# Attention and a two-layer network on one core: nine chunks of 512 tokens in place of 36 of 128, longer load rows, and a hand-set order

## The chip, the cores and the metric

One core of one Trainium2 chip. The metric is the device time of one execution in microseconds (us), lower is better. Every kernel below ran several times, on the same chip and in the same session as the kernel before it. The sessions were on different chips, and the kernel before took 407.98 to 409.81 us in them, so a difference of 1 or 2 us between medians of two sessions says nothing; there the ratios are to be compared.

Names in the profiles: PE is TensorE, which multiplies matrices, PEld its weight loads; DVE is the vector engine, ACT the scalar engine, POOL GpSimd, and SP the sync engine, which here only issues loads and stores. A "y copy" is DVE's copy of a finished y out of the buffer that TensorE writes to.

## The reference, cut to what matters

```python
batch, n_heads, seq, head_dim = 8, 8, 576, 64
n_tokens, d_model, d_ff = 4608, 512, 2048
q_s = np.exp(q - np.max(q, axis=-1, keepdims=True)); q_s = q_s / (np.sum(q_s, axis=-1, keepdims=True) + 1e-09)
k_s = np.exp(k - np.max(k, axis=2, keepdims=True));  k_s = k_s / (np.sum(k_s, axis=2, keepdims=True) + 1e-09)
kv = np.einsum('bhsd,bhse->bhde', k_s, v)             # one 64x64 matrix per head
attn_out = np.einsum('bhsd,bhde->bhse', q_s, kv)
x = attn_out.transpose(0, 2, 1, 3).reshape(B * S, H * D)
h = x @ w_in
g = 0.5 * h * (1.0 + erf(h * inv_sqrt2))
out = g @ w_out
```

There are some 36.7 MB to read and 9.4 MB to write. Nearly all the arithmetic is in the two products of the network, called h and y below. Attention is the part before them; its "kv step" makes the small matrix of each head.

## The kernel before

The network runs in 36 chunks of 128 tokens. In a chunk, four quarters of h (16 matmuls of 128 columns each) alternate with GELU on the scalar engine and four y matmuls of 512 columns. A scheduler chooses the order of instructions on every engine. All input loads are issued from POOL in rows of 256 bytes (64 floats of one head), and the weights pass through two staging buffers of 512 KB.

```python
def load_weights():
    for i in range(NDM):
        for hlf in range(2):
            wtmp = f32in.tile([128, DF // 2], FP32, tag="wtmp")      # pool with bufs=2
            nc.gpsimd.dma_start(out=wtmp, in_=moe_w_in[...])
            nc.scalar.copy(out=wi_bf[:, i, ...], in_=wtmp)
    # ... w_out the same way, cast by nc.vector
def moe_chunk(tcn):
    cols = slice(tcn * 128, (tcn + 1) * 128)
    for qt in range(NQT):                                  # four quarters
        h_ps = psum_m.tile([128, 4, 128], FP32, tag="h", bufs=2)
        for j in range(4):
            t = qt * 4 + j
            for dm in range(NDM):
                nc.tensor.matmul(h_ps[:, j, :], wi_bf[:, dm, t*128:(t+1)*128], xT[dm][:, cols], ...)
        nc.scalar.activation(out=g[:, qt*4:(qt+1)*4, :], in_=h_ps, func=AF.Gelu)
        for j in range(4):
            nc.tensor.matmul(y_ps, g[:, qt*4+j, :], wo_bf[:, qt*4+j, :], ...)
    nc.vector.tensor_copy(out=y_sb, in_=y_ps)
    nc.sync.dma_start(out=out[cols, :], in_=y_sb)
def load_bhsd(dst, src_b, engine):                         # engine: nc.gpsimd
    for c in range(C):                                     # rows of 64 floats
        engine.dma_start(out=dst[:, c, :, :], in_=src_b[:, s0:s0+128, :].rearrange("h p d -> p h d"))
# ... attn_batch(b): exp, sums, multiply by 1/sum, kv step, transposes, products (cut)
```

The softmax here doesn't subtract the row's maximum and nothing guards it: scores larger than these inputs give would overflow.

## Time and profile before

| | before |
|---|---|
| time, median of 4 runs of the session that compared the two | 407.98 us |
| profiled span | 409.1 us |
| TensorE matmuls | 3488 records, busy 84% of the span |
| first GELU | 50.2 us |
| one undisturbed chunk of 128 tokens | 8.08 us |

The page of the kernel before, its slices: the span is cut into 40 equal parts of 10.2 us, each digit is the busy share of a part in tenths, PEclk the granted TensorE clock in tenths, and GB/s what the DMA engines moved.

```profile
span 409.1 us, 7832 instructions
...
PE   0073378998799999999889899999999999989995
...
PEclk9999998996899999999989999999999999999998
...
GB/s 152 218 149 236 207 246 243 229 237 170 137 239 64 203 232 119 239 110 212 221 117 242 88 44 36 28 26 53 27 27 26 53 27 27 27 26 27 27 34 44
...
PE 46%; ACT 21%; DMA 13%; POOL 11%; DVE 5%; issue 4%; ACTq 0%; POOLq 0%
```

TensorE (PE) does nothing in the first two slices (20 us), has 3 to 7 tenths in the next four, where it works on the attention of the first batch and waits for weights, and is at 0.8 or 0.9 nearly everywhere after that. A digit of 9 doesn't say that the engine is at its best. The last line is the share of each engine in the chain of waits that ended last: ACT has 21% of it, in a kernel whose matmuls should bound it. Where it enters is seen in the timeline of one quarter. Columns: start, duration, engine, line and operation, output and inputs, count; in brackets the idle time of the engine before it and what ended it.

```profile
401.49 0.60 ACT L93 ACTIVATE g<-h_ps 128x512 bf16<-128x512 f32 x1 [1.41 <-PE h_ps L86]
402.14 0.55 PEld L98 LDWEIGHTS <-g 128*128 128x128 bf16 x4 [0.25 <-ACT g L93]
402.15 1.04 PE L98 MATMUL y_ps<-wo_bf,g 128*128 128x512 bf16 x4
402.81 0.48 PEld L86 LDWEIGHTS <-wi_bf 128*128 128x128 bf16 x5
403.02 0.44 PE L86 MATMUL h_ps<-xT,wi_bf 128*128 128x128 bf16 x5
403.50 0.60 ACT L93 ACTIVATE g<-h_ps 128x512 bf16<-128x512 f32 x1 [1.41 <-PE h_ps L86]
404.15 0.55 PEld L98 LDWEIGHTS <-g 128*128 128x128 bf16 x4 [0.86 <-ACT g L93]
```

The five h matmuls at 403.02 are the last of their group of 16; the scheduler had put the other eleven ahead of the y group before. Only after them can GELU start (403.50), and y's weight load (404.15) waits for it to end. This is the end of the kernel, with no h left to do in the meantime, and the wait is 0.86 us. Everywhere else eleven matmuls of the next group fill 11 x 56 ns = 0.62 us of it, and about 0.25 us remain, as at 402.14: in the undisturbed stretch 0.25 to 0.31 us in each quarter of 2.007 us. Its sum is in the list of waits (columns: who waits, for what, total us, times, longest).

```profile
PEld L98 <- ACT g L93: 33.5, 110, 2.5
```

### The profile page before, as it was taken

What the parts mean: (1) busy time and instruction counts of PE and PEld (TensorE: products, weight loads), DVE (VectorE), ACT (ScalarE), POOL (GpSimd) and SP (SyncE); (2) the same over time, 40 slices, a digit from 0 to 9 for tenths busy, and PEclk for the clock granted to TensorE, in tenths of its full rate; (3) what the DMA queues carried; (4) which work ended last, traced back from release to release, by engine and by line L of the source; (5) the groups of instructions that cost most, each with busy time, mean ns of one, the idle gap of its engine ahead of it and who ended that gap; (6) DMA issues with size and microseconds to landing.
All of it is one profiled execution on the core that took longest, in us unless ns stands there. A gap on an engine that the chain in (4) does not pass through costs nothing.

```text
span 409.1 us, 7832 instructions
## 1 busy us (share of the span) xinstructions
PE 341.9 (84%) x3488; PEld 228.1 (56%) x3488; DVE 122.9 (30%) x228; ACT 168.7 (41%) x198; POOL 161.4 (39%) x158
## 2 busy tenths in 40 slices
PE   0073378998799999999889899999999999989995
PEld 0041257565466665666646566666666666656663
DVE  0352034256337173490741830011001000250010
ACT  0523563645475293762845822223332322212221
POOL 9753336993955949759397210000000000000000
PEclk9999998996899999999989999999999999999998
DMA  6947678996592894948949310001000100000001
GB/s 152 218 149 236 207 246 243 229 237 170 137 239 64 203 232 119 239 110 212 221 117 242 88 44 36 28 26 53 27 27 26 53 27 27 27 26 27 27 34 44
DMA packets 17121, 49.79 MB, mean 122 GB/s; under 512 B 2752, under 2 KB 2752, under 8 KB 17088
## 3 DMA queue, kind: packets, MB, share of 16 engines
q0 software_dynamic: 11904, 39.85, 39.8%
q1 hardware_dynamic: 5184, 9.44, 6.3%
q8 instruction: 27, 0.44, 0.5%
q14 instruction: 6, 0.05, 0.0%
HBM read 39.85 MB, written 9.44 MB: 120 GB/s over the span
## 4 chain that ended last, share of the span: by engine, by line
PE 46%; ACT 21%; DMA 13%; POOL 11%; DVE 5%; issue 4%; ACTq 0%; POOLq 0%
PE y_ps L98 29%; ACT g L93 15%; PE h_ps L86 11%; DMA wtmp<-in_moe_w_in_dram 5%; PE kv_ps L155 3%; POOL qf L112 3%; POOL qs L139 3%; DMA wtmp<-in_moe_w_out_dram 3%; DMA qf<-in_q_dram 3%; POOL vf L112 2%; DMA vf<-in_v_dram 2%; POOL kf L112 2%; PE ot L182 1%; DVE qsum L136 1%; ACT L93 1%
## 5 line engine op out<-in xcount | busy, mean ns | idle before, releaser
L86 PEld LDWEIGHTS <-wi_bf 128*128 128x128 bf16 x2304 | 145.9, 101 | 48.8 <-ACT wi_bf L60 12.2
L86 PE MATMUL h_ps<-xT,wi_bf 128*128 128x128 bf16 x2304 | 158.6, 224 | 15.2 <-ACT wi_bf L60 11.1
L98 PE MATMUL y_ps<-wo_bf,g 128*128 128x512 bf16 x576 | 150.2, 388 | 17.7 <-ACT g L93 5.1
L93 ACT ACTIVATE g<-h_ps 128x512 bf16<-128x512 f32 x144 | 84.5, 597 | 186.6 <-PE h_ps L86 186.4
L98 PEld LDWEIGHTS <-g 128*128 128x128 bf16 x576 | 47.3, 99 | 76.8 <-ACT g L93 33.5
L106 DVE COPY y_sb<-y_ps 128x512 f32<-128x512 f32 x36 | 24.9, 691 | 186.5 <-PE y_ps L98 186.5
L139 POOL TENSOR_TENSOR qs<-eq,recq 128x2560 bf16<-128x2560 bf16 x8 | 35.8, 4474 | 45.8 <-DVE recq L137 39.5
L112 POOL DMA_DIRECT2D qf<-in_q_dram x40 | 40.8, 1024 | 0.3 <-issue 0.3
L112 POOL DMA_DIRECT2D kf<-in_k_dram x40 | 36.2, 913 | 0.7 <-issue 0.7
L112 POOL DMA_DIRECT2D vf<-in_v_dram x40 | 35.2, 887 | 1.8 <-PE ot L182 1.0
L167 PE MATMUL tp<-identity,qs 128*128 128x128 bf16 x128 | 14.1, 232 | 22.3 <-POOL qs L139 22.3
L188 DVE CAST xT<-ot 128x288 bf16<-128x288 f32 x64 | 26.3, 452 | 12.5 <-PE ot L182 12.2
L155 PE MATMUL kv_ps<-v_aug,ek 128*64 128x65 bf16 (+1 forms) x320 | 28.6, 211 | 0.1
L136 DVE TENSOR_REDUCE qsum<-eq 128x40 f32<-128x2560 bf16 x8 | 22.4, 2805 | 14.3 <-ACT eq L127 14.3
L155 PEld LDWEIGHTS <-ek 128*64 128x64 bf16 (+1 forms) x320 | 20.7, 114 | 10.5 <-issue 5.1
L182 PE MATMUL ot<-qsT,kvn 64*64 64x288 bf16 x128 | 15.5, 321 | 8.1 <-DVE kvn L162 7.9
L167 PEld LDWEIGHTS <-qs 128*128 128x128 bf16 x128 | 7.8, 101 | 24.6 <-POOL qs L139 22.3
L93 ACT ACT_TABLE_LOAD x15 | 19.2, 1283 | 5.2 <-PE h_ps L86 5.0
L128 ACT ACTIVATE ek<-kf 128x2560 bf16<-128x2560 f32 x8 | 18.7, 2337 | 2.4 <-DMA kf<-in_k_dram 2.4
L132 DVE CAST v_aug<-vf 128x2560 bf16<-128x2560 f32 x8 | 17.0, 2130 | 6.7 <-DMA vf<-in_v_dram 6.7
L127 ACT ACTIVATE eq<-qf 128x2560 bf16<-128x2560 f32 x8 | 18.7, 2337 | 0.1
L127 ACT ACT_TABLE_LOAD x8 | 10.3, 1283 | 18.1 <-DMA qf<-in_q_dram 18.0
(19 smaller groups left out, 83.5 us busy)
## 6 DMA issues: line engine op xcount, KB each, us to landing
qf<-in_q_dram POOLq DMA_DIRECT2D x40, 256.0 KB, 4.9
kf<-in_k_dram POOLq DMA_DIRECT2D x40, 256.0 KB, 6.8
vf<-in_v_dram POOLq DMA_DIRECT2D x40, 256.0 KB, 8.6
out_dram<-y_sb SPq DMA_DIRECT2D x36, 256.0 KB, 2.1
wtmp<-in_moe_w_in_dram POOLq DMA_DIRECT2D x8, 512.0 KB, 4.9
wtmp<-in_moe_w_out_dram POOLq DMA_DIRECT2D x8, 512.0 KB, 4.3
```

Of the source, the lines that this page charges most:

```text
L86: nc.tensor.matmul(h_ps[:, j, :], wi_bf[:, dm, t * 128:(t + 1) * 128], xT[dm][:, cols], start=(dm == 0), stop=(dm == NDM - 1),)
L93: nc.scalar.activation(out=g[:, qt * 4:(qt + 1) * 4, :], in_=h_ps, func=AF.Gelu)
L98: nc.tensor.matmul(y_ps, g[:, t, :], wo_bf[:, t, :], start=(t == 0), stop=(t == NDF - 1),)
L106: nc.vector.tensor_copy(out=y_sb, in_=y_ps)
L112: engine.dma_start(out=dst[:, c, :, :], in_=src_b[:, s0:s0 + 128, :].rearrange("h p d -> p h d"),)
L127: nc.scalar.activation(out=eq, in_=qf, func=AF.Exp)
L136: nc.vector.reduce_sum(out=qsum, in_=eq, axis=mybir.AxisListType.X)
L139: nc.gpsimd.tensor_tensor(out=qs, in0=eq, in1=recq.to_broadcast([128, C, H, D]), op=mybir.AluOpType.mult,)
L155: nc.tensor.matmul(kv_ps[pb:pb + 64, :], lhsT, rhs, start=(c == 0), stop=(c == C - 1),)
L167: nc.tensor.transpose(tp[:, c * 128:(c + 1) * 128], qs_flat[:, c, h0 * D:(h0 + 2) * D], identity,)
L182: nc.tensor.matmul(ot[pb:pb + 64, :], kvn[pb:pb + 64, :], qsT[pb:pb + 64, ssl], start=True, stop=True,)
L188: nc.vector.tensor_copy(out=xT[hp][:, b * S + half * 288: b * S + (half + 1) * 288], in_=ot,)
```

## The change

Its intent: (1) work on 512 tokens at a time, h for all 16 groups first, then y for four times 128 tokens, with three h buffers; (2) let a partition hold four neighbouring tokens, so that a load row is 1 KB (the token order is permuted inside a chunk and undone by the store); the last 64 tokens of each batch become a ninth chunk; (3) issue all loads from SP; weights in 1 MB pieces; (4) the two heads of a pair in one kv matmul; (5) switch the scheduler off and set the order on every engine by hand. Cut to its core:

```diff
+    ctx.enter_context(tc.manual_schedule())
+    src = q[b, :, 0:M, :].rearrange("h (p j) d -> p h (j d)", j=J)         # J = 4, M = 512
+    nc.sync.dma_start(out=qf[:, i*n:(i+1)*n, :], in_=src[:, i*n:(i+1)*n, :])
+    def h_phase(c, ins):
+        for t in range(NDF):
+            ps = psum_h.tile([128, M], FP32, tag="h")                      # bufs=3
+            for dm in range(NDM):
+                nc.tensor.matmul(ps, wi_bf[:, dm, t*128:(t+1)*128], xT[:, dm, :], ...)
+            nc.scalar.activation(out=g[:, t, :], in_=ps, func=AF.Gelu)
+            for f in ins.get(t, []): f()                # work set in after group t
+    def y_phase(c, ins):
+        for j in range(J):
+            for t in range(NDF):
+                nc.tensor.matmul(ps, g[:, t, j*128:(j+1)*128], wo_bf[:, t, :], ...)
+                for f in ins.get((j, t), []): f()
+            nc.vector.tensor_copy(out=y_sb, in_=ps)     # then the store
+    wst = ctx.enter_context(tc.tile_pool(name="wst", bufs=2))              # weight staging, 1 MB
+    h_phase(0, ins_h0)
+    exp_k(1); exp_q(1); table(AF.Gelu)
+    y_phase(0, {
+        (0, 15): [lambda: load_q(2), lambda: load_kv(2)],
+        (1, 15): [lambda: norm_q(1, parts=2, engs=[nc.gpsimd, nc.vector]), lambda: cast_v(1)],
+        (2, 15): [lambda: kv_step(1, 0), lambda: kv_step(1, 1), lambda: tp_step(1, 0), lambda: tp_step(1, 1)],
+        (3, 7): [lambda hp=hp: x_step(1, hp, ...) for hp in range(HP)],
+    })
+    # ... chunk 1 alike; for chunks 2 to 8 the attention of the next chunk is set into h,
+    #     and its sums and v cast into y at (1, 15)
-    # ... moe_chunk, load_bhsd, attn_batch, load_weights as above
```

## The prediction

> **What bounds it now.** TensorE, in three stretches (stretch table and timeline):
> - 0 to 50 us: no bulk matmuls. Exp starts at 10.7 us; weights come as 512 KB loads through two buffers (4.7 us from issue to landing); first GELU at 50.2 us. The first loads run at about 215 GB/s (256-byte rows), the DMA engines 85% busy.
> - 50 to about 200 us: 128-token chunks mixed with attention and waits; POOL (120 input-load issues of 0.9 us, 4.5 us multiplies) and DMA are busy.
> - The pure stretch: a chunk takes 8.08 us (y copies at 332.42 and 340.51). A quarter of it is 2.007 us: 16 h matmuls at 56 ns and 4 y matmuls at 217 ns are 1.77; the rest is y's weight load waiting 0.25 to 0.31 us for GELU. 36 x 8.08 = 291 us.
>
> **After (estimates from these rates).** 1152 matmuls of 512 columns at 217 ns, each with its own weight load as y has today: 250 us. The bubble (0.25 x 144 = 36 us) should vanish: GELU takes 0.60 us, four matmuls 0.87, with three PSUM buffers. Attention: about 3.2 us a batch (20 kv matmuls, 16 transposes, 4 of 512), 23 us beyond the start. The Trainium skill ("TensorE: Matmul & The Clock Gate", Part 1) gives 215.7 and 55.6 ns for warm matmuls of 512 and 128 columns; the trace agrees within 1%. So width alone saves nothing; the bubble and the schedule do.
>
> **Start.** 3.4 MB of q, k, v in 1 KB rows: I estimate 300 GB/s (between today's 215 and up to 340 in the weight stretch), v landed at 13 to 15 us, first weights at 17 to 18, then casts and x evictions: h starts at about 21 us, in place of 50. A cold clock costs 1 to 2 us.
>
> **New waits.** (a) Chunk 0's y: batch 1's loads sit on SP behind weight loads that wait for casts and land near 50 us; exps, sums and the v cast follow (2.3, 2.8, 2.1 us for 2560 columns, times 0.8). TensorE, in order, waits about 9 us at batch 1's kv step. (b) Chunk 1's y: batch 2's exps start only after the last GELU; about 6 us at its kv step. (c) Chunks 2 to 5: the DVE block (sums, v cast) stands ahead of the second y copy, whose buffer the fourth y group needs: 1.8 us each, 7 us. (d) Late w_out in chunk 0: 0 to 2 us.
>
> **Sum.** 21 + 1.5 + 250 + 23 + 9 + 6 + 7 + tail 4 (today 3.9 from the last y matmul to the end) = 321; some waits may be hidden: **318 us**, range **302 to 340** (8 in 10). Faster by over 2%: 0.97; within 2%: 0.02; slower: 0.01. Of the 89 us gained, 29 come from the start, 36 from the bubble, the rest from attention waiting less.
>
> **Right if:** first GELU at 20 to 24 us; h and y matmuls at 217 ns in runs of 64; an undisturbed chunk of 27.8 us plus 3.2 of attention; the waits list shows TensorE waiting for DVE (v cast, y copies) some 20 us in all, mostly before 110 us; about 300 GB/s in the first 14 us.
>
> **Wrong if:** 512-column h matmuls don't hide their weight loads; y waits for its chunk's last GELU (0.7 us x 9); 1 KB loads are slower, or SP issues them slowly; the clock drops in the long waits; or POOL and DVE slow each other (the v cast took 1.50 us alone, 2.13 on average).

## The result, and the profile after

326.56 us median of 4 runs, against 407.98 us. The ratio is 0.7984, 95% interval 0.7951 to 0.8017. Here and below a ratio is the mean time of one kernel's fast runs over that of the kernel before in the same rounds, so it isn't quite the ratio of the medians.

The same lines of the page, after (a slice is now 8.1 us):

```profile
span 324.5 us, 3715 instructions
...
PE   0499774799939999999999998999899999999994
...
PEclk9999969599969999999999999999999999999999
...
GB/s 226 329 282 337 306 287 295 298 129 265 95 32 67 162 280 44 65 200 254 34 67 275 177 34 93 283 143 33 105 123 1 65 67 0 26 73 32 0 67 65
...
PE 63%; DVE 11%; ACT 10%; DMA 10%; issue 3%; SPq 2%; POOL 0%; DVEq 0%; ACTq 0%
```

TensorE begins in the second slice, and ACT's share of the chain has fallen from 21 to 10%. But DVE's share has gone from 5 to 11%, and the granted clock drops to 0.6 and 0.5 of full in the sixth and eighth slice and to 0.6 in the twelfth. After the first slice, the loads run at about 300 GB/s (282 to 337) through the eighth; before, no slice had more than 250. The start is now full of data. The table of stretches shows where: start; h of chunk 0; y of chunk 0; chunk 1; chunk 2; chunk 3. Columns: the stretch, its length, busy time of PE, its weight loads, DVE, ACT and POOL, each with its count of instructions, granted clock, DMA share, GB/s.

```profile
0.00:20.00 20.00, 6.83 (x41) 4.14 (x42) 10.95 (x26) 9.68 (x12) 8.37 (x19) 1.00 0.90 275
20.00:35.20 15.20, 15.10 (x62) 6.54 (x64) 4.90 (x6) 10.24 (x17) 2.98 (x2) 1.00 0.86 307
35.20:68.20 33.00, 21.75 (x104) 11.10 (x104) 13.74 (x24) 8.90 (x10) 5.16 (x4) 0.79 0.99 280
68.20:106.60 38.40, 32.41 (x167) 16.14 (x168) 14.23 (x25) 20.67 (x25) 1.90 (x1) 0.91 0.42 117
106.60:137.80 31.20, 30.68 (x167) 15.04 (x169) 16.63 (x26) 16.55 (x22) 9.42 (x2) 1.00 0.51 143
137.80:169.40 31.60, 30.79 (x167) 15.05 (x169) 12.79 (x23) 16.55 (x22) 4.71 (x1) 1.00 0.51 142
```

A chunk with attention needs, by the rates of the prediction, 27.8 + 3.2 = 31.0 us; chunks 2 and 3 take 31.2 and 31.6. But y of chunk 0 with the attention of batch 1 takes 33.0 us where 13.9 + 3.2 = 17.1 would do, and chunk 1 takes 38.4. What TensorE waited for (the dots stand for 9.3 us at the start, for POOL's multiply of the first q):

```profile
PE ps L181 <- DVE v_aug L158: 14.0, 3, 6.2
...
PE ps L254 <- POOL wo_bf L301: 4.6, 2, 2.6
PE ps L254 <- DVE y_sb L261: 2.9, 4, 1.0
```

14.0 us for casts of v (2.3 at the start, 6.2 in chunk 0, 5.5 in chunk 1), 4.6 us for w_out, 2.9 us for y copies. And the timeline of TensorE in y of chunk 0 shows what follows the waits:

```profile
35.29 1.89 PE L254 MATMUL ps<-wo_bf,g 128*128 128x512 bf16 x8
39.17 1.02 PE L254 MATMUL ps<-wo_bf,g 128*128 128x512 bf16 x4 [2.00 <-POOL wo_bf L301]
42.76 10.01 PE L254 MATMUL ps<-wo_bf,g 128*128 128x512 bf16 x35 [2.56 <-POOL wo_bf L301]
59.01 0.59 PE L181 MATMUL ps<-v_aug,ek 128*128 128x130 bf16 x4 [6.23 <-DVE v_aug L158]
...
61.12 1.91 PE L210 MATMUL ps<-identity,eq 128*128 128x128 bf16 x16
...
99.20 1.06 PE L210 MATMUL ps<-identity,eq 128*128 128x128 bf16 x16
```

In brackets is what ended each wait. The same instructions are faster elsewhere: 16 transposes take 1.91 us at 61.12 us and 1.06 us at 99.20 us. The trace has the granted clock at 0.50 in three stretches of 6.83 us, from 40.18, 57.24 and 91.38 us, and at full between them. At the start, too, matmuls were slow: the weight loads of the first h matmuls, one to each, stand 0.43 us apart until 23.2 us. The table reads a clock of 1.00 there only because the trace has no record of the clock before 23.11 us.

```profile
20.30 0.15 PEld L241 LDWEIGHTS <-wi_bf 128*128 128x128 bf16 x1 [0.28 <-issue]
20.73 0.15 PEld L241 LDWEIGHTS <-wi_bf 128*128 128x128 bf16 x1 [0.28 <-issue]
21.15 0.15 PEld L241 LDWEIGHTS <-wi_bf 128*128 128x128 bf16 x1 [0.28 <-issue]
```

### The profile page after: what moved, and what is told of

It is laid out like the page before. It is cut to its first block, busy times and chain, and to the rows that moved or that the text cites. A ratio compares the mean times of both kernels' runs of the same rounds, so it can differ in the third digit from the quotient of the medians.

```text
span 324.5 us, 3715 instructions
## 1 busy us (share of the span) xinstructions
PE 285.2 (88%) x1490; PEld 139.4 (43%) x1520; DVE 120.0 (37%) x207; ACT 149.0 (46%) x202; POOL 45.6 (14%) x31
## 4 chain that ended last, share of the span: by engine, by line
PE 63%; DVE 11%; ACT 10%; DMA 10%; issue 3%; SPq 2%; POOL 0%; DVEq 0%; ACTq 0%
PE ps L241 34%; PE ps L254 21%; DVE qsum L168 4%; DMA f<-in_k_dram 4%; ACT ek L148 3%; ACT eq L136 3%; PE ps L181 3%; PE ps L210 3%; DMA f<-in_v_dram 2%; DVE v_aug L158 2%; PE ps L222 2%; ACT L143 2%; DMA w<-in_moe_w_in_dram 2%; DMA w<-in_moe_w_out_dram 2%; DVE y_sb L261 1%
## 5 line engine op out<-in xcount | busy, mean ns | idle before, releaser
L245 ACT ACTIVATE g<-ps 128x512 bf16<-128x512 f32 x144 | 86.0, 597 | 123.9 <-PE ps L241 123.2
L254 PE MATMUL ps<-wo_bf,g 128*128 128x512 bf16 x564 | 130.0, 386 | 8.0 <-POOL wo_bf L301 4.6
L241 PE MATMUL ps<-xT,wi_bf 128*128 128x512 bf16 x558 | 133.1, 382 | 1.0 <-DVE xT L230 0.2
L241 PEld LDWEIGHTS <-wi_bf 128*128 128x128 bf16 x576 | 55.5, 98 | 64.0 <-issue 3.4
L170 POOL TENSOR_TENSOR eq<-eq,recq 128x2048 bf16<-128x2048 bf16 (+1 forms) x9 | 32.9, 3651 | 186.1 <-DVE recq L169 167.6
L261 DVE COPY y_sb<-ps 128x512 f32<-128x512 f32 x36 | 24.4, 686 | 90.7 <-PE ps L254 78.2
L168 DVE TENSOR_REDUCE qsum<-eq 128x16 f32<-128x1024 bf16 (+1 forms) x12 | 20.9, 1743 | 39.3 <-ACT eq L136 39.1
L230 DVE CAST xT<-ps 128x512 bf16<-128x512 f32 x32 | 21.6, 689 | 22.3 <-PE ps L222 18.9
L148 ACT ACTIVATE ek<-f 128x2048 bf16<-128x2048 f32 (+1 forms) x9 | 15.4, 1708 | 4.1 <-DMA f<-in_k_dram 4.1
L136 ACT ACTIVATE eq<-qf 128x2048 bf16<-128x2048 f32 (+1 forms) x9 | 15.4, 1707 | 2.9 <-DMA qf<-in_q_dram 2.9
```

Source lines behind the costliest of these rows:

```text
L136: nc.scalar.activation(out=dst[:, i * n:(i + 1) * n], in_=src[:, i * n:(i + 1) * n], func=AF.Exp)
L148: nc.scalar.activation(out=dst[:, i * n:(i + 1) * n], in_=src[:, i * n:(i + 1) * n], func=AF.Exp)
L168: nc.vector.reduce_sum(out=qsum[:, :, hs], in_=eq[:, :, hs, :], axis=AX.X)
L170: engs[i % len(engs)].tensor_tensor(out=eq[:, :, hs, :], in0=eq[:, :, hs, :], in1=recq[:, :, hs].unsqueeze(3).to_broadcast([128, J, n, D]) ...
L230: nc.vector.tensor_copy(out=st[b]["xT"][:, hp, :], in_=ps)
L241: nc.tensor.matmul(ps, wi_bf[:, dm, t * 128:(t + 1) * 128], xT[:, dm, :], start=(dm == 0), stop=(dm == NDM - 1),)
```

## The experiments

Twelve kernels ran, all correct. "b_" ones alter the kernel before, "a_" ones the kernel after.

### b_lead: the gap between GELU and y, mended in the kernel before

```diff
             nc.scalar.activation(out=g[:, qt*4:(qt+1)*4, :], in_=h_ps, func=AF.Gelu)
-            for j in range(4): nc.tensor.matmul(y_ps, ...)
+            if pend: pend.pop()()                       # the y quarter before this one
+            pend.append(lambda qt=qt: y_quarter(qt, g, y_ps, cols))
```

> The kernel before, with one thing changed: the four y matmuls of a quarter are traced after all 16 h matmuls of the next quarter (before, the scheduler put only 11 of those 16 ahead of them, so they came 0.6 us after the GELU began and waited 0.25 us). Theory A (the bubble between GELU and y is 0.25 us x 144 = 36 us of the gain, whatever the width of the matmuls): the pure stretch falls from 8.08 to about 7.1 us a chunk, PE's wait for GELU in front of y nearly vanishes, and the whole falls from 408 to 372-385 us, the full 36 only if the attention half is bound by TensorE as well. Rival B (the bubble is hidden elsewhere, or the gain of the change comes from the 512-wide matmuls themselves): the chunk stays near 8 us and the time over 400 us.

384.76 us, ratio 0.9382 (0.9325 to 0.944): about 25 us less. Timeline of b_lead in its undisturbed stretch:

```profile
333.96 1.09 PEld L100 LDWEIGHTS <-wi_bf 128*128 128x128 bf16 x16
334.18 1.06 PE L100 MATMUL h_ps<-xT,wi_bf 128*128 128x128 bf16 x16
335.02 0.59 PEld L82 LDWEIGHTS <-g 128*128 128x128 bf16 x4
335.07 1.03 PE L82 MATMUL y_ps<-wo_bf,g 128*128 128x512 bf16 x4
335.27 0.60 ACT L107 ACTIVATE g<-h_ps 128x512 bf16<-128x512 f32 x1 [1.21 <-PE h_ps L100]
```

All 16 h matmuls now stand in front of the y group, and y's weight load at 335.02 shows no wait. A chunk takes 7.07 us (y copies at 325.50 and 332.57). The list of waits of b_lead, to be held against 33.5 us before:

```profile
PEld L82 <- ACT g L107: 9.7, 10, 2.9
```

So 23.8 us of waiting went, and the kernel became 25 us faster. Theory A holds, and the prediction's 36 us (0.25 us times all 144 quarters) was too much: only 110 quarters waited, and ten still do.

### b_lead_w6: and six staging buffers for the weights

```diff
-            wtmp = f32in.tile([128, DF // 2], FP32, tag="wtmp")
+            wtmp = f32in.tile([128, DF // 2], FP32, tag="wtmp", bufs=6)    # and for w_out
```

> The kernel before with y a quarter later, as in the first run of this study (384.8 us), and six staging buffers for weights in place of two. Theory A (the start of the kernel before is a ring: two 512 KB buffers, 4.7 us from issue to landing, then a cast; bytes alone would allow half the time): first GELU at 36-42 us and not 50, and 376-380 us in all. Rival B (the start is bound elsewhere, or what it gains is lost again because the attention of the next batches then lacks data): first GELU may move, but the time stays at 383-387 us.

370.27 us, ratio 0.9044 (0.9019 to 0.9069), 14 us below b_lead; first GELU at 39.8 us. That is 6 us better than theory A's range. So the two-buffer ring cost the kernel before about 14 us, once the gap was mended. Two small repairs of the old kernel, with no change of layout or width, give 39 of the 81 us.

### b_sp: all loads from SP in the kernel before

```diff
-    nc.gpsimd.dma_start(...)        # 120 input loads and 16 weight loads
+    nc.sync.dma_start(...)
```

> The kernel before, with all input loads issued from SP and not from POOL; rows (256 bytes) and buffers as they were. Theory A (half of the 29 us that the start loses is the weight loads standing behind POOL's 4.5 us multiply and its 0.9 us issues, the rest is two 512 KB buffers in a ring and the order of casts): first GELU at 38-45 us and not 50, and the attention half a little faster because POOL no longer issues 120 loads: 395-402 us in all. Rival B (the start is bound by bytes alone): first GELU stays within 3 us of 50 and the time within 1% of 408. A possible loss: stores and loads share one in-order queue, which may make loads wait for stores.

414.92 us, ratio 1.0123 (1.0066 to 1.0181): a miss. That is within the 2% which the record still calls the same, but the interval lies above 1. The first GELU came at 43.8 us, as theory A had it, but the kernel was slower. By the times of the y copies it led until the 16th (232.8 against 235.8 us) and fell behind at the 17th (250.7 against 243.5). The possible loss named in the expectation fits: stores that wait for y copies (217.8 us in SP's own list of waits) stand in the same in-order queue as loads. The trace shows a chain of this kind for the last batch: the fifth load of q leaves SP at 221.31 us, right after a store (220.91) that had waited for the y copy at 220.19, where the kernel before had issued it by 212.4 us; exp, sum and multiply of that q follow, TensorE waits 1.96 us for the multiply (until 238.67), and the clock is at 0.50 from 238.74 to 248.98 us. No run isolates what this is worth, so that it makes up the loss stays an inference. What is shown is that moving the loads to SP is not by itself a gain.

### a_narrow: h with 128-column matmuls in the kernel after

```diff
-            for dm in range(NDM):
-                nc.tensor.matmul(ps, wi_bf[...], xT[:, dm, :], ...)
+            for j in range(J):
+                js = slice(j * 128, (j + 1) * 128)
+                for dm in range(NDM):
+                    nc.tensor.matmul(ps[:, js], wi_bf[...], xT[:, dm, js], ...)
```

> The kernel after, with h made of 128-column matmuls again (four for each of 512 columns), in the same order, layout and buffers. Theory A (width saves nothing by itself beyond the 2 to 3 ns that each matmul adds: 4 x 56 against 217 ns): 64 more matmul groups of 7 ns, about 4-5 us on the whole, so 329-333 us against 326.6, still 19% below before. Rival B (the wide matmul is what pays, since each 128-column matmul must load its own weights): a large part of the 81 us comes back, 345 us or more.

330.82 us, ratio 0.8082 (0.8039 to 0.8126), 4 us more than the kernel after. Width is worth about 1% here. The weight loads are 213.3 us busy against 139.4, and hidden all the same.

### a_rows256: rows of 256 bytes in the kernel after

```diff
-    src = q[b, :, 0:M, :].rearrange("h (p j) d -> p h (j d)", j=J)
+    src = q[b, :, 0:M, :].rearrange("h (j p) d -> p h j d", j=J)           # one DMA a head
```

> The kernel after, with the token order not permuted: rows of 256 bytes again for q, k and v (each load of one head its own DMA, since the pattern has a dimension more), all else as it is. Theory A (1 KB rows matter only in the first 50 us, where the loads of batches 0 and 1 stand on the path): at about 215 GB/s the first h begins 4-6 us later (24-26 us and not 20) and batch 1 lands some 4 us later, so 332-340 us. Rival B (rows don't matter, bytes do): within 2 us of 326.6. Rival C (issue cost on SP or contention of slow loads reaches the steady part): over 345 us, with waits after 110 us.

333.22 us, ratio 0.8137 (0.8092 to 0.8181), 6 to 7 us more; first h at 24.5 us and not 19.9. The DMA view of the first 14 us in 40 slices of 0.35 us, first the kernel after, then a_rows256:

```profile
GB/s 0 0 0 0 0 99 120 290 380 389 378 380 380 353 286 294 220 178 203 202 319 348 351 369 354 342 301 274 207 217 211 178 301 342 348 354 342 375 342 395
DMA packets 4341, 3.65 MB, mean 261 GB/s; under 512 B 1152, under 2 KB 4224, under 8 KB 4341
```

```profile
GB/s 0 0 0 0 0 113 235 155 233 246 236 233 231 250 231 219 228 249 129 109 217 245 214 187 240 233 232 253 231 244 194 238 212 236 182 192 194 179 204 217
```

Rows of 1 KB run mostly at 340 to 390 GB/s, those of 256 bytes at 180 to 250. The dips to 180 to 220 in the first list follow the loads of the last 64 tokens of k and v, which still have 256-byte rows; but by the packets of the trace most of those rows had moved in the slices just before, and in the dips it is 1 KB packets that take 72 to 100 ns in place of 46. Why is open.

The edit changes a second thing: each load becomes one DMA a head, and SP needs 4.30 us to issue the eight of q, 0.54 us for each 128 KB, which alone would allow only some 244 GB/s. The packets show that the rows count all the same: one of 256 bytes took 18 ns, and one of 1 KB 46 ns in the stretch at 380 GB/s (medians), and the DMA engines were 0.9 busy or more in most slices. What the issues would cost by themselves was not tested. The Trainium skill ("DMA: Bandwidth & Descriptors", section "Why small descriptors are slow (HBM only)") names a fixed cost of about 3 cycles per packet beside 8 for 256 bytes, an overhead of 27%. Against rows of 1 KB, which bear the 3 cycles too, an estimate from that page is 11 cycles to 8.75 for 256 bytes, a loss of 20%. The direction agrees; the loss measured here, 380 against some 235 GB/s or 38%, is larger. Theory A holds: the rows matter at the start and for batch 1. The h of chunk 1 begins at 74.97 us, 6.7 later than in the kernel after, and that of chunk 2 at 113.01, 6.4 later, so nothing more is lost after that.

### a_warm: useless matmuls in the waits

```diff
+    def warm(b, n):
+        ps = psum_a.tile([128, M], FP32, tag="a", name="dummy")            # never read
+        for i in range(n): nc.tensor.matmul(ps, identity, st[b]["xT"][:, 0, :], start=True, stop=True)
     y_phase(0, {
+        (0, 7): [lambda: warm(0, 8)], (0, 11): [lambda: warm(0, 10)],
-        (2, 15): [lambda: kv_step(1, 0), ...
+        (2, 15): [lambda: warm(0, 24), lambda: kv_step(1, 0), ...          # and 22 in chunk 1
```

> The kernel after, with idle TensorE time filled by matmuls whose results nobody reads (8 and 10 of 512 columns where y of chunk 0 waits for w_out, 24 ahead of the kv step of batch 1, 22 ahead of that of batch 2), sized to end before the wait does. They do no useful work and take away no wait. Theory A (each wait [...] is followed by 3 to 4 us at half the granted clock, by the trace about 5 us lost in y of chunk 0 and 2 us in y of chunk 1): the granted clock stays full there, the matmuls after the waits stand 217 ns apart and not 427, and 4-7 us are gained: 320-323 us. Rival B (the slow stretches come from something else, such as DMA traffic on the memory, or the end of batch 1's data sets the time anyway): within 1.5 us of 326.6, or slower.

323.3 us, ratio 0.7889 (0.7866 to 0.7913): 3 us less by the medians, 4 by the ratios, with 64 more matmuls. This lies between the two theories, nearer to A. The timeline of TensorE in a_warm, same stretch as above:

```profile
44.66 7.93 PE L259 MATMUL ps<-wo_bf,g 128*128 128x512 bf16 x35 [1.40 <-POOL wo_bf L306]
52.42 5.34 PE L237 MATMUL dummy<-xT,identity 128*128 128x512 bf16 x24
60.76 0.39 PE L181 MATMUL ps<-v_aug,ek 128*128 128x130 bf16 x4 [2.99 <-DVE v_aug L158]
...
68.04 2.32 PE L246 MATMUL ps<-xT,wi_bf 128*128 128x512 bf16 x10
```

The 35 y matmuls take 7.93 us where the kernel after took 10.01, and four kv matmuls 0.39 us against 0.59; the mean granted clock is 1.000 against 0.967. So the slow stretches are the clock, and idle time brings them on. But the first 2.1 us won do not count: the kv step waits for batch 1 either way. In this execution, moreover, batch 1 came later: one of the loads of w_out landed 2 us late, before the first useless matmul had run, the loads of batch 1 behind it left SP as much later, and the kv step began at 60.76 us and not 59.01. So h of chunk 1 starts at 68.04 us, hardly before the kernel after's 68.28. What was won lies behind the waits: 7.3 us from the kv step to h of chunk 1 against 9.3, and 36.7 us for chunk 1 against 38.4. What counts is the clock after the last wait of a chunk.

The Trainium skill ("TensorE: Matmul & The Clock Gate", Part 1) says that the clock is halved after an idle window of about 3.4 us and comes back after a busy one. The trace agrees with half speed (427 ns a matmul from 42.76 to 46.98 us), and its stretches at half clock last 6.83 us, twice the 3.41 us of the shortest in other runs (a_narrow, from 95.97 us). But no wait as long as 3.4 us was needed: the clock fell at 40.18 us, after one wait of 2.00 us and 1.02 us of work, before the wait of 2.56 us began. And a wait of 2.99 us in a_warm (up to 60.76 us) left it at full. So the length of a single wait doesn't decide it; no run here isolates what does.

### a_front: another order on DVE

```diff
-        (1, 15): [lambda: norm_q(1, ...), lambda: cast_v(1)],
+        (1, 15): [lambda: cast_v(1), lambda: norm_q(1, ...)],              # chunk 0
-        (0, 15): [lambda: norm_q(2, ...), lambda: cast_v(2)],
+        (0, 15): [lambda: cast_v(2)], (1, 0): [lambda: norm_q(2, ...)],    # chunk 1
-            yi[(1, 15)] = [lambda nb=nb: dve_front(nb)]
+            yi[(2, 0)] = [lambda nb=nb: dve_front(nb)]                     # chunks 2 and on
```

> The kernel after with the order on DVE changed only: the cast of v stands ahead of the sums and the multiply of q for batches 1 and 2, and the block for batches 3 and later stands after the second y copy and not before it. Theory A (the kv steps of batches 1 and 2 and the fourth y group wait for this order: 6.2 + 5.5 + 2.9 us, and each long wait costs about 2 us more in a half-rate clock after it): kv waits fall to about 1-3 us and 0-1 us, y copy waits to 0, the clock stays up in the second chunk: 313-319 us. Rival B (those waits are really for data or for exp on ACT): less than 4 us gained.

316.65 us, ratio 0.7746 (0.7699 to 0.7792), 10 us less: theory A. The waits for y copies are gone and chunk 1 is 5.5 us shorter. In chunk 0, however, nothing was gained, h of chunk 1 starting at 68.49 us. There the wait only moved, and the clock was at half for 10.24 us (56.36 to 66.60) where the kernel after had 6.83. TensorE's waits in a_front:

```profile
PE ps L210 <- POOL eq L170: 11.4, 2, 9.3
PE ps L181 <- DVE v_aug L158: 4.6, 2, 2.6
PE ps L254 <- POOL wo_bf L301: 4.2, 2, 2.7
PE ps L210 <- DVE kvbd L197: 3.0, 2, 1.6
```

The kv steps wait less (4.6 us against 14.0), but the transposes behind them now wait: 2.2 us more for POOL's multiply and 3.0 us for buffers that DVE has yet to empty.

### a_wst: four staging buffers in the kernel after

```diff
-    wst = ctx.enter_context(tc.tile_pool(name="wst", bufs=2))
+    wst = ctx.enter_context(tc.tile_pool(name="wst", bufs=4))
```

> The kernel after with four staging buffers for the weights in place of two. Theory A (the second half of w_out is late because its loads wait for casts to free a buffer, 4.6 us of TensorE waits plus about 2 us of half-rate clock, and batch 1 lies behind them on SP): waits for w_out vanish, batch 1 lands 1-3 us earlier, 318-323 us. Rival B (the start up to 55 us is bound by bytes: the DMA engines are 90-99% busy from 20 to 68 us): the w_out wait goes, but batch 1 lands no earlier, so the kv wait of batch 1 grows by as much: within 2 us of 326.6.

321.8 us, ratio 0.7874 (0.7831 to 0.7917), 5 us less. The waits for w_out are gone, the kv wait of batch 1 grew from 6.2 to 8.2 us, and h of chunk 1 starts at 63.7 us. Theory A holds in the main: the weights came earlier, and so did batch 1 (the multiply of its q on POOL starts at 50.59 us and not at 54.50), against theory B; but TensorE was there earlier still and gave 2 us back waiting for it.

### a_best: both

```diff
+    # a_front and a_wst together
```

> Both of the last two together: DVE order and four staging buffers. If the parts are independent: their gains add up, 306-313 us. If batch 1's bytes bound the first 55 us: no better than the DVE order alone by more than 2 us.

312.86 us, ratio 0.7648 (0.76 to 0.7695), 14 us less: the gains nearly add up (10 + 5). h of chunk 1 now starts at 61.87 us, 6.4 us earlier than in the change, where a_front alone gave nothing and a_wst alone 4.6.

### a_sched: the scheduler's order for the changed kernel

```diff
-    ctx.enter_context(tc.manual_schedule())
```

> The kernel after without its hand-set order: the scheduler orders the same instructions by its own priorities (it mixes h of one chunk into y of the one before, and takes the exps early between GELUs). Theory A (the hand order is worth little: layout, buffers and the phase structure give the gain): 320-335 us. Rival B (the hand order is what pays: scheduler puts exps and table loads between GELUs and stalls h): 340-370 us, with more table loads than 18 and TensorE waiting for GELU.

316.74 us, ratio 0.775 (0.7704 to 0.7796), below the range of both theories: the scheduler's order beats the hand-set one by 10 us. It loads ACT's tables more often (34 times against 16), and h groups wait 5.5 us for GELU, but its longest kv wait is 2.8 us and its mean clock 0.995 (0.967 in the change), and h of chunk 1 begins at 60.0 us. So the hand-set order, as the change had it, cost time.

### a_best2: the mended order

```diff
-    exp_k(1); exp_q(1); table(AF.Gelu)
+    exp_q(1); exp_k(1); table(AF.Gelu)
     y_phase(0, {
-        (1, 15): [lambda: norm_q(1, ...), lambda: cast_v(1)],
-        (2, 15): [kv_step(1, 0), kv_step(1, 1), tp_step(1, 0), tp_step(1, 1)],
-        (3, 7): [x_step ...]
+        (1, 0): [lambda: norm_q(1, ...)],
+        (2, 0): [lambda: cast_v(1)],
+        (2, 15): [tp_step(1, 0), tp_step(1, 1)],
+        (3, 7): [kv_step(1, 0), kv_step(1, 1)],
+        (3, 15): [x_step ...]                # four staging buffers; (2, 0) for later chunks
         # chunk 1: cast_v(2) at (0, 0), norm_q(2) at (1, 0), tp_step at (2, 15), x_step at (3, 15)
```

> A version meant to beat all: the kernel after with four staging buffers, exp of q ahead of exp of k for batches 1 and 2, sums and multiply of q as soon as q's exp is there, the cast of v apart from it, kv steps in the middle of the last y group, and the DVE block of batches 3 and later behind the second y copy. If the remaining waits of the last combination (2.8 us kv, 3.0 and 2.2 us transposes, in y of chunk 0; 1.4 in y of chunk 1) are matters of order: 303-307 us, first h of chunk 1 at 54-56 us and not 61.9. If bytes bind there (batch 1's v lands at 47.7 us): 308-312 us.

302.85 us, ratio 0.7391 (0.7374 to 0.7407), the fastest of all: 24 us below the change. h of chunk 1 starts at 54.75 us. The mean granted clock is 1.000. TensorE's waits in a_best2:

```profile
PE ps L210 <- POOL eq L170: 9.3, 1, 9.3
PE ps L181 <- DVE v_aug L158: 2.3, 1, 2.3
PE ps L254 <- POOL wo_bf L301: 1.3, 1, 1.3
PE ps L181 <- DVE qT L215: 0.8, 1, 0.8
```

The first, second and last lines are the start, before the first h. After it, one wait of 1.3 us for w_out is left and no other over 0.5 us. What was done is to let each piece of DVE and ACT work of batch 1 start when its data lands (q before k before v) and to put into TensorE's stream last what depends on the last to land.

### a_sched_wst: the scheduler's order for that version

```diff
-    ctx.enter_context(tc.manual_schedule())      # in a_best2
```

> The version of the run just named, with the scheduler's order in place of the hand-set one. If the scheduler is as good as a mended hand order: within 3 us of it. If its advantage over the change was only that it stepped around the three waits, it now has none and loses by its extra table loads and the h groups that wait for GELU (5.5 us before): 308-314 us.

315.86 us, ratio 0.7713 (0.7684 to 0.7742), as good as a_sched and 13 us behind the mended hand order. Its range was 308 to 314, a narrow miss, so the scheduler profits less from the better parts than expected: h still waits 3.7 us for GELU and a kv step 2.7 us for v.

## Why the prediction was right, and where its sizes were off

Predicted were 318 us, 302 to 340; measured 326.56 us (profiled 324.5). Point by point:

- **The start.** Right. Predicted: h at 21 us, v landed at 13 to 15, weights cast from 17 to 18. The second half of v was cast from 14.52 us, the first weights from 17.24, h began at 19.92, GELU at 21.8. 300 GB/s was predicted; 3.65 MB in the first 14 us, of which the first 1.75 were empty, are 298 GB/s. The first GELU came 28.4 us earlier than before; that 29 us of the gain come from the start, as the prediction says, no run isolates. The weight ring of the kernel before was part of what the start lost: its removal alone gave 14 us (b_lead_w6).
- **250 us of h and y, 23 us of attention.** Right: chunks 2 and 3 take 31.2 and 31.6 us against 31.0.
- **"Width alone saves nothing."** Nearly right: 4 us (a_narrow), what 576 wide matmuls make at 4 x 56 - 217 = 7 ns each.
- **36 us from the bubble.** The mechanism was right, the size a third too large: 25 us (b_lead). The step that failed is the multiplication by all 144 quarters; the list of waits would have given 33.5 us in 110, of which 23.8 can be had.
- **Waits.** (a) 9 predicted, 6.2 found; (b) 6 and 5.5; (c) 7 and 2.9, the v cast being faster (1.21 us) than the mean it was scaled from; (d) 0 to 2 and 4.6. Their sum was right, 22 to 24 against 19.2, but in part by luck: (c) was too much by 4.1 us and (d) too little by 2.6 or more. a_front, a_wst and a_best show that they are what the text says they are. What the text did not see is that the waits in chunk 0 have two causes one behind the other, order and staging, and that the order alone, taken away, gains nothing in chunk 0, staging alone 4.6 us and both 6.4.
- **The clock.** This is the term of the sum that was mis-sized: 1 to 2 us at the start were put in, and the drop in the long waits stood only among what could go wrong. The slow stretches cost about 2 us each in three places (y and the kv steps of chunk 0, kv steps of chunk 1). Of these 6 us only 3 to 4 come back when the clock is kept up (a_warm), because the first stretch lies in front of a wait for data.
- **The difference in all.** 326.56 - 318 is 8.6 us. The prediction's sum was 321 and 3 were taken off for waits that might be hidden, which they were not. The profiled span is 3.5 us over that sum: about 6 more for the clock, 3 less for the waits, 1 less for the start, and the rest in short waits and the tail (4.7 us from the last y copy's start, 319.82, to the end, against 4). The timed runs are another 2 us over the profiled one.

Of the 81 us gained, the runs account for 25 (bubble) and 14 (weight ring) in the kernel before, and show that 6 to 7 us of the whole depend on the rows (with the number of DMAs) and 4 on the width. These may overlap, so they are not to be summed; how the rest divides among POOL freed of loads, the new attention and the chunk structure stays open. The hand-set order took about 10 us away (a_sched).

## What to carry to other kernels

Before a wider operation is costed, see whether the narrow one already runs at its rate: here the loss lay in a 0.25 us gap that the scheduler made, and a reordering in the old kernel got 25 us back. When order is set by hand, list for every in-order engine what stands in front of the instruction that others wait for; one block ahead of a copy, or a load behind a waiting store, can cost at every chunk. Waits of a few microseconds on TensorE can cost a second time where the half-rate clock afterwards lies on the critical path, so after mending one wait look at where TensorE waits next before counting the gain.

## What the Trainium skill lacked or had wrong

- "TensorE: Matmul & The Clock Gate", Part 1, lets the clock fall after an idle window of about 3.4 us and gives no length for shorter waits. Here one wait of 2.00 us with 1.02 us of work after it was enough (clock at 0.50 from 40.18 us), while a wait of 2.99 us in a_warm and one of 1.33 us in a_best2 left the clock at 1.00.
- The same page warns that a profile's records of the clock can be unreliable, but has no remark that they can begin late: the first one of the kernel after is at 23.11 us, so the stretch from 20 to 35.2 us reads 1.00, while the first matmuls of h stood 427 ns apart (20.30 to 22.86 us).
- "DMA: Bandwidth & Descriptors" gives 27% as the overhead of 256-byte descriptors, by an estimate from it 20% against 1 KB; about 235 against 380 GB/s, 38%, was measured here on loads from SP, with packets of 18 and 46 ns.
- No page says what it costs to put loads and stores on one issuing engine whose stores wait for results; b_sp lost 1% by it or beside it, after a start 6 us faster.
